# Attention with an MLP on one core: the turns of a step moved behind the second MLP unit of their gap, four idle matmuls removed

## The chip, the cores and the metric

One core of one Trainium2 chip. Times are device microseconds (us) of one execution, as the median of several. In a trace, PE is TensorE (PEld its weight loads), DVE is VectorE, ACT is ScalarE, POOL is GpSimd. Shorter is better; a difference under 2% counts as "same".

## The reference

Eight batches, twelve heads, 448 tokens, head size 64. Queries and keys are normalised, attention is taken, the heads are joined and go through an MLP.

```python
q_n, k_n = rmsnorm(q, g_q), rmsnorm(k, g_k)              # (8, 12, 448, 64)
attn = softmax(q_n @ k_n.T / 8)
x = (attn @ v).transpose(0, 2, 1, 3).reshape(3584, 768)
h = x @ w_in                                             # 768 -> 2048
g = max(h, 0) + alpha * min(h, 0)
out = g @ w_out                                          # 2048 -> 768, float32
```

## The kernel before

The heads of a batch are done in three steps of four heads, so there are 24 steps (y = 0 to 23). A step has seven score tiles. The program is a hand-made order of 66 bursts: each issues two or three score tiles with their exponentials, at times the denominators (`den`) or the outputs (`attv`) of an earlier step, and is followed by a gap that holds MLP units of an earlier batch: `up` (6 matmuls into one bank, then gT = max(h, alpha h) by ScalarE and VectorE) and `down` (16 matmuls). The order of the program is the order on each engine.

A *turn* makes a step's keys ready. Up to step 7, TensorE transposes q and k, and VectorE copies both out of PSUM, the memory that TensorE writes. From step 8 on DMAs have transposed them, and the turn is one VectorE instruction that scales kT in place:

```python
def turn(y):
    if y >= TD:                                   # TD = 8
        t = qkT[y, "k"].rearrange("p j g c -> p (j g c)")
        nc.vector.tensor_scalar(                  # 128x896 fp16, SBUF to SBUF (L179)
            out=t, in0=t, scalar1=gain[:, 0:1], scalar2=None, op0=ALU.mult
        )
        return
    ...                                           # 14 transposes (L193), then
    ...                                           # qT by a copy (L202), kT scaled by gain (L204)

def square(y, nm):                                # of a later step, by GpSimd
    ...
    nc.gpsimd.tensor_mul(out=sqf, in0=src, in1=src)                    # L135

def scale(y, nm):                                 # of a later step, mostly by GpSimd
    ...
    eng.tensor_mul(out=..., in0=nat[y, nm], in1=rr_t[y]...)            # qs, L158
```

The loop over bursts, as far as it matters (n is the burst; `turns[n]` is the step whose turn lies in its gap, mostly one burst before that step's first score):

```python
for n in range(NB):
    ...                                           # scores, exponentials, den / attv
    for k, (f, a) in enumerate(gaps[n]):
        spare = k == spare_at                     # this unit goes into the accumulator's banks
        if f is down:
            down(*a, jobs.pop(n, ()), spare)
        else:
            f(*a, spare)
            ...
        if k == 0 and n in turns:
            turn(turns[n])
    if not gaps[n] and n in turns:
        turn(turns[n])
    ...
    if n < first and plain and n not in turns:    # first = 12
        spin(4)                                   # four matmuls on zeros, to keep TensorE busy
    elif lead and n in dens:
        spin(8)
```

## Time and profile before

| | kernel before |
|---|---|
| time, median of 3 | 453.33 us (452.82 to 453.57) |
| PE busy in the profiled run | 426.9 of 451.6 us |
| ACT, DVE, POOL busy | 290.0, 207.8, 171.2 us |
| granted TensorE clock | 0.999 |

(The profiled run, 453.43 us, is a further one.)

TensorE is busy nearly all the time, so its waits are what to look for. The list of waits of the kernel before has these rows for the keys (columns: who waited, for whom; us in total, times, longest):

```profile
PEld L217 <- DVE kT L204: 4.0, 4, 1.3
PE sc L217 <- DVE kT L204: 3.2, 4, 1.0
PEld L217 <- DVE kT L179: 0.5, 1, 0.5
```

The first two are the opening's, where each step's keys are made just in time. Of the 16 turns that only scale kT (L179), one made a weight load wait, for half a microsecond.

### The profile page before, as it was taken

To read this page: it belongs to the slowest core of one execution; us is meant where nothing else is said; L and a number is where in the kernel's file an instruction comes from. 1 tells how busy PE (TensorE), PEld (TensorE's weight loads), DVE (VectorE), ACT (ScalarE), POOL (GpSimd) and SP (SyncE) were. 2 spreads that over 40 slices of the span, in tenths; PEclk is the share of its full clock that TensorE was granted. 3 is DMA by queue.
4 is the path that set the end of the run, shared out by engine and by line. 5 is a ranking of instruction groups with operands and counts; after the bars stand their busy time and mean duration, and the time that the engine had idled before them with its cause. 6 is when DMAs were issued, how large, how long until landed. Compare 5 with 4: busy or idle time off the path is not lost.

```text
span 451.6 us, 9099 instructions
## 1 busy us (share of the span) xinstructions
PE 426.9 (95%) x3848; PEld 230.0 (51%) x3848; DVE 207.8 (46%) x297; ACT 290.0 (64%) x401; POOL 171.2 (38%) x125
## 2 busy tenths in 40 slices
PE   8768989899999999999999999999999999999996
PEld 3334544555445545455545545455555555455563
DVE  3655553635463544444563544444563343343421
ACT  4998789557875848558785848558785846423300
POOL 5779952751472350750572350750542000000000
PEclk9999999999999999999999999999999999999999
DMA  8999995484655642764664642764361510111122
GB/s 191 233 247 241 232 240 117 60 168 110 158 94 127 159 105 53 140 156 118 157 109 111 158 107 53 139 157 118 77 100 38 77 37 1 37 35 36 35 71 70
DMA packets 60009, 52.77 MB, mean 117 GB/s; under 512 B 32688, under 2 KB 56512, under 8 KB 59968
## 3 DMA queue, kind: packets, MB, share of 16 engines
q1 hardware_dynamic: 47424, 39.27, 36.9%
q0 software_dynamic: 11808, 11.81, 16.7%
q10 hardware_dynamic: 736, 1.11, 1.0%
q8 instruction: 30, 0.49, 0.5%
q14 instruction: 11, 0.09, 0.1%
HBM read 45.62 MB, written 11.01 MB: 125 GB/s over the span
## 4 chain that ended last, share of the span: by engine, by line
PE 79%; ACT 14%; DVE 4%; DMA 1%; issue 1%; SPq 0%; ACTq 0%
PE op L301 31%; PE hT L284 18%; PE hTa L284 9%; ACT expT L229 8%; PE sc L217 7%; PE av L240 5%; PE dn L240 5%; ACT ah L292 2%; PE opa L301 2%; ACT rden L255 2%; DVE gT L293 2%; ACT rden L260 1%; DMA nat<-in_k_dram 1%; PE tps L193 1%; DVE ss L141 1%
## 5 line engine op out<-in xcount | busy, mean ns | idle before, releaser
L229 ACT ACTIVATE expT<-sc,expb 128x896 f16<-128x896 f32 x168 | 157.6, 1008 | 18.9 <-PE sc L217 18.7
L301 PE MATMUL op<-w_out_sb,gT 128*128 128x384 f16 x848 | 145.9, 326 | 2.1 <-DVE gT L293 2.0
L158 POOL TENSOR_TENSOR qs<-nat,rr 128x896 f16<-128x896 f32 x44 | 78.3, 1799 | 177.7 <-issue 159.0
L284 PE MATMUL hT<-xT,w_in_sb 128*128 128x448 f16 x558 | 117.1, 353 | 2.7 <-DVE gT L293 2.6
L301 PEld LDWEIGHTS <-gT 128*128 128x128 f16 x896 | 84.6, 98 | 65.5 <-issue 12.3
L284 PEld LDWEIGHTS <-w_in_sb 128*128 128x128 f16 x768 | 73.7, 98 | 72.8 <-issue 8.5
L292 ACT ACTIVATE ah<-hT,cols 128x448 f16<-128x448 f32 x93 | 59.1, 636 | 59.5 <-PE hT L284 59.4
L293 DVE TENSOR_TENSOR gT<-hT,ah 128x448 f16<-128x448 f32 x93 | 58.0, 624 | 76.5 <-ACT ah L292 76.5
L135 POOL TENSOR_TENSOR sq<-nat 128x896 f32<-128x896 f32 x44 | 73.0, 1681 | 1.4 <-DMA nat<-in_q_dram 1.3
L313 DVE COPY osb<-op 128x384 f32<-128x384 f32 x53 | 29.5, 557 | 89.4 <-PE op L301 89.4
L217 PE MATMUL sc<-qT,kT 64*64 64x448 f16 x672 | 53.2, 359 | 9.5 <-ACT expT L229 6.0
L292 ACT ACTIVATE ah<-hTa,cols 128x448 f16<-128x448 f32 x35 | 22.2, 633 | 49.5 <-PE hTa L284 49.5
L141 DVE TENSOR_REDUCE ss<-sq 128x14 f32<-128x896 f32 x48 | 49.8, 1076 | 6.5 <-ACT sq L133 6.1
L284 PE MATMUL hTa<-xT,w_in_sb 128*128 128x448 f16 x210 | 45.4, 352 | 0.0
L217 PEld LDWEIGHTS <-kT 64*64 64x64 f16 x672 | 19.2, 104 | 39.1 <-issue 29.0
L240 PE MATMUL av<-expT,vt 64*64 64x448 f16 x672 | 36.0, 350 | 2.2 <-ACT rden L255 2.2
L293 DVE TENSOR_TENSOR gT<-hTa,ah 128x448 f16<-128x448 f32 x35 | 21.8, 623 | 31.3 <-ACT ah L292 31.3
L240 PE MATMUL dn<-expT,ones 64*64 64x448 f16 x672 | 35.9, 349 | 0.2 <-DVE gT L293 0.2
L268 DVE TENSOR_TENSOR xT<-av,rden 128x896 f16<-128x896 f32 x24 | 26.2, 1090 | 20.7 <-PE av L240 20.7
L240 PEld LDWEIGHTS <-vt 64*64 64x64 f16 x672 | 20.3, 107 | 14.3 <-issue 3.7
L240 PEld LDWEIGHTS <-ones 64*64 64x64 f16 x672 | 20.5, 107 | 11.9 <-issue 1.0
L260 ACT ACTIVATE rden<-rden 128x896 f32<-128x896 f32 x24 | 23.0, 957 | 0.6
(37 smaller groups left out, 134.0 us busy)
## 6 DMA issues: line engine op xcount, KB each, us to landing
out_dram<-osb SPq DMA_DIRECT2D x54, 192.0 KB, 2.7
nat<-in_q_dram SPq DMA_DIRECT2D x46, 224.0 KB, 6.1
nat<-in_k_dram SPq DMA_DIRECT2D x46, 224.0 KB, 6.9
vt<-in_v_dram POOLq DMA_DIRECT2D x16, 336.0 KB, 7.6
w_in_sb<-in_moe_w_in_dram POOLq DMA_DIRECT2D x4, 768.0 KB, 13.2
w_out_sb<-in_moe_w_out_dram POOLq DMA_DIRECT2D x4, 768.0 KB, 16.6
nat<-in_q_dram ACTq DMA_DIRECT2D x2, 224.0 KB, 4.6
nat<-in_k_dram ACTq DMA_DIRECT2D x2, 224.0 KB, 6.1
```

What stands on the lines that cost most here:

```text
L135: nc.gpsimd.tensor_mul(out=sqf, in0=src, in1=src)
L141: nc.vector.tensor_reduce(out=ss_t[y][:, "qk".index(nm)].rearrange("p h j -> p (h j)").unsqueeze(2), in_=sqs[y, nm], axis=AXIS_X, op=ALU.add,)
L158: eng.tensor_mul(out=t.rearrange("p j h d -> p h j d"), in0=nat[y, nm], in1=rr_t[y][:, "qk".index(nm)].unsqueeze(3).broadcast_to((128, 2, ...
L217: nc.tensor.matmul(out=sc[ds(64 * g, 64), par, :S].rearrange("p (j c) -> p j c", j=J), lhsT=kT[ds(64 * par, 64), j, g, :], rhs=qT[ds(64 * ...
L229: nc.scalar.activation(out=expT[y][:, j], in_=scs[y, j][:, :, :S], func=AF.Exp, scale=QK_SCALE, bias=expb[:, 0:1],)
L240: nc.tensor.matmul(out=acc[ds(64 * par, 64), g, :S], lhsT=weights(g, par, j), rhs=e[ds(64 * g, 64), j, par, :], start=(j == 0), stop=(j == ...
L260: nc.scalar.activation(out=r, in_=r, func=AF.Exp, scale=-1.0)
L284: nc.tensor.matmul(out=hT[:, :S], lhsT=w_in_sb[:, c, ts(ft, 128)], rhs=x[:, c, :], start=(c == order[0]), stop=(c == order[-1]),)
L292: nc.scalar.activation(out=ah, in_=hT[:, :S], func=AF.Copy, scale=alpha_sb[:, ft : ft + 1])
L293: nc.vector.tensor_max(out=gT[:, ft, ds((b & 1) * S, S)], in0=hT[:, :S], in1=ah)
L301: nc.tensor.matmul(out=op[:, :OH], lhsT=gT[:, ft, ts(t, 128)], rhs=w_out_sb[:, ft, ds(oh * OH, OH)], start=(ft == 0), stop=(ft == NF - 1),)
L313: nc.vector.tensor_copy(out=o[:, ds(oh * OH, OH)], in_=op[:, :OH])
```

## The change

The intent, as the change states it: let the first units of a gap go ahead of the turn, and do away with idle matmuls where TensorE is about to do the third group's denominators.

```diff
-            if k == 0 and n in turns:
-                turn(turns[n])
+            if k == min(1, len(gaps[n]) - 2) or len(gaps[n]) == 1:
+                if n in turns:
+                    turn(turns[n])
         if not gaps[n] and n in turns:
             turn(turns[n])
         for _, g, c in late:
             g(*c)
-        if n < first and plain and n not in turns:
+        if n < den_at[G - 1] - 1 and plain and n not in turns:
             spin(4)
```

A gap of three or more units now has its turn behind the second; a gap of two keeps it behind the first. The second edit takes out one group of four idle matmuls, that of burst 10.

## The prediction

> **What bounds the kernel now.** The program runs in bursts of two or three score tiles, each followed by a gap that holds MLP units (up: 6 matmuls, down: 16) and at times the turn of a step, which readies its keys. I read the page's chain first, then TensorE's timeline, then VectorE's and GpSimd's beside it. The chain that ended last:
>
> ```profile
> PE 79%; ACT 14%; DVE 4%; DMA 1%; issue 1%; SPq 0%; ACTq 0%
> ```
>
> TensorE holds 79% of it, and PE is busy 426.9 of 451.6 us. In its timeline nearly all its pauses lie before 127 us (the opening and the first bursts with MLP work, where ScalarE's exponentials lead) or near 385. From 127 to 385 us it runs almost without a gap, so there anything that makes TensorE wait goes into the total. One of the change's 14 moved places, as the trace has it: step 10 of 24 (eight batches, three groups of heads each; TensorE, then VectorE, then GpSimd):
>
> ```profile
> 142.44 2.77 PE L301 MATMUL op<-w_out_sb,gT 128*128 128x384 f16 x16
> 145.05 1.30 PE L284 MATMUL hTa<-xT,w_in_sb 128*128 128x448 f16 x6
> 146.18 1.30 PE L284 MATMUL hT<-xT,w_in_sb 128*128 128x448 f16 x6
> 147.41 0.57 PE L217 MATMUL sc<-qT,kT 64*64 64x448 f16 x8
> ```
>
> ```profile
> 145.25 0.56 DVE L313 COPY osb<-op 128x384 f32<-128x384 f32 x1 [1.72 <-PE op L301]
> 145.73 0.47 DVE L179 TENSOR_SCALAR kT<-kT,gain 128x896 f16<-128x896 f16 x1
> 147.05 0.62 DVE L293 TENSOR_TENSOR gT<-hTa,ah 128x448 f16<-128x448 f32 x1 [0.86 <-ACT ah L292]
> 148.19 0.62 DVE L293 TENSOR_TENSOR gT<-hT,ah 128x448 f16<-128x448 f32 x1 [0.51 <-ACT ah L292]
> ```
>
> ```profile
> 144.25 3.48 POOL L158 TENSOR_TENSOR qs<-nat,rr 128x896 f16<-128x896 f32 x2 [10.52 <-issue]
> 147.70 3.31 POOL L135 TENSOR_TENSOR sq<-nat 128x896 f32<-128x896 f32 x2
> ```
>
> The gap is one down unit and two up units, then the scores at 147.41, which read this kT. The turn of a step from 8 on is only VectorE's scaling of kT. It stands behind the down unit, is done at 146.19, and the scores have 1.2 us to spare. It fills VectorE's idle time before gT, which waits for ScalarE either way.
>
> **What the Trainium skill says.** "SBUF — State Buffer", Who interferes with whom: VectorE's second port pair is GpSimd's, taken exclusively for a whole instruction; tensor_scalar in a two-port mode takes it, and the other "fully blocks". The trace agrees closely:
>
> ```profile
> L179 DVE TENSOR_SCALAR kT<-kT,gain x16: 445/658/975, 112.9 to 362.9; 128x896 f16<-128x896 f16 x16
> ```
>
> The 445 ns is the one where GpSimd is idle. The others (466, 658, 971) start at different points within the first qs, but all end 0.25 us after that qs ends (145.94 to 146.19; 127.31 to 127.56), and the second qs then takes 1837 instead of 1687 ns. "VectorE: DVE Perf Modes", Mode 4×_2P: four elements a cycle for this form; 896 / 4 / 0.96 GHz = 233 ns, the 0.25 us. "TensorE: Matmul & The Clock Gate", Part 3, The mechanism: matmuls start in strict program order, so a score that waits holds all behind it; TensorE's timeline shows no overtaking. The same page, Part 1: the clock falls after an idle window of about 3.4 us; granted clock here is 1.00 from 134 to 236 us, and no new wait that I expect reaches that.
>
> **The change part by part.** The order of VectorE's instructions confirms: of the gaps with three or more units, 14 hold a turn; 13 of them move one kT scaling behind one more gT, and step 4 moves 14 transposes and two copies. Gaps of two units or none are as before. All other engines keep their order, except the four idle matmuls taken out.
>
> *Idle matmuls (39 us).* They cost 0.86 us on the chain, but what follows does not only wait for them:
>
> ```profile
> 38.99 0.93 PE L328 MATMUL spin<-idle,ident 128*128 128x448 f16 x4
> 39.85 1.52 PE L240 MATMUL dn<-expT,ones 64*64 64x448 f16 x28
> 40.64 0.32 ACT L152 ACTIVATE rr<-ss,epsb 128x28 f32<-128x28 f32 x1 [0.52 <-DVE ss L141]
> 40.99 0.23 ACT L153 ACTIVATE rr<-rr 128x28 f32<-128x28 f32 x1
> 41.42 0.92 ACT L255 ACTIVATE rden<-dn 128x896 f32<-128x896 f32 x1 [0.20 <-PE dn L240]
> ```
>
> The logarithm of the denominators (41.42) stands behind the two root instructions, which wait for VectorE's sums and end at 41.22. It can move up 0.2 us at most: **-0.2 us**.
>
> *Step 4 (51 to 56 us).* Now: transposes 51.62, qT 53.03, kT 53.56, scores 54.77. After: the second unit takes the transposes' place; its gT comes at 53.92 (ah behind the exponential that ends 53.35), qT 0.54 later, kT 0.54 after that, done 55.67, scores 55.72: 0.95 late. The exponential behind them starts at 55.41 now (behind ah of the third unit) and would start 0.43 after the scores, 56.15. From here ScalarE's chain leads: **+0.7**.
>
> *Steps 10, 12, 14, 16, 18, 20, 22* (scores first in the next burst). kT follows gT by 0.54 us (126.05 to 126.59 at step 9) and takes 0.445 if free; TensorE resumes 0.045 later. Step 10: 147.05 + 0.54 + 0.445 + 0.045 = 148.08 against 147.41, +0.67. But GpSimd must be asked. qs starts at 144.25, its second ends 147.59 when nothing disturbs it, and the square starts 147.55; kT starts at 147.586. From the waits above I work out, as an estimate, that kT needs the ports some 0.2 us after its recorded start and a GpSimd instruction 0.14 us after its own. So the square has them 0.09 us earlier, and kT waits until it ends, 149.22, + 0.25: scores at 149.52, **+2.1**. Step 16 has the same distances (qs 245.84, gT 248.64): +2.1. At steps 12, 14, 18 and 20 gT comes 2.60 us after qs instead of 2.80, and kT asks just as the second qs ends: +0.67 each; for 12 and 18 the down unit of the next gap already waits 1.02 us for gT behind the exponentials, so only their delay, about 0.47, counts. Step 22 meets no later GpSimd work: +0.67. Sum 2×2.1 + 2×0.47 + 3×0.67 = **+7.1**.
>
> *Steps 11, 17, 23* (scores second in the burst, 0.2 us later). gT 161.04 gives kT done 162.02, scores 162.07 against 161.60: 3×0.46 = **+1.4**.
>
> *Steps 9, 15, 21* (gap of up units). One or two units still follow the turn, so alone it costs nothing. At 15 kT would start at 228.58, against 228.55 of the second qs: loses the ports by the same 0.08 us, ends 230.24 + 0.25, scores 230.54 against 229.74: +0.8; step 21 the same. Step 9 starts 0.07 ahead of the qs and wins by a hair: 0. **+1.6**.
>
> Sum: -0.2 + 0.7 + 7.1 + 1.4 + 1.6 = +10.6 us on 453.3: 463.9. The gT that come up to 0.7 us sooner gain nothing: where TensorE waits for gT (126.7, 189.0), it is one ahead of the turn or behind ScalarE.
>
> **The rivals.**
> (a) The same delays, but kT gets the ports at steps 10, 15, 16 and 21, my margin being 0.08 us from two recorded starts and an estimated offset. Then 2×0.67 in place of 2×2.1 and 0 for 1.6: +6.2, 459.5 us. For it: recorded starts of GpSimd are rough. Against it: distances that repeat to 10 ns at steps 10 and 16.
> (b) Step 9 loses the ports too: +1.1, 465.0.
> (c) It gains: the idle matmuls' 0.86 us is wholly given back and gT, sooner, frees the hT banks. For it: they are on the chain of waits. Against it: the roots end 0.2 us ahead of the logarithm, and bank waits of moved gaps are before the turn. It would make 452.5.
> (d) The delays are caught up later by slack. Against it: TensorE is gapless where they fall. With half absorbed: 458.5.
>
> **Range and chances.** 2% is 462.4 us. I give my base case with or without (b) some 0.63, (a) 0.3 with mixtures near the line, (c) 0.01. Predicted 463.6, pulled a little down by (a); range 459.0 to 465.4. Faster 0.01, same 0.37, slower 0.62.
>
> **What would show it.** Right: a new wait of the score's weight load for kT L179, about 12 times, 7 to 11 us in total; two of some 2.1 us, two of 0.8, the rest 0.45 to 0.67; kT scalings of about 1.9 us at steps 10, 15, 16 and 21; the logarithm no more than 0.2 us sooner; score waits for kT L204 grown by one near 55 us. Wrong in size: kT there at 0.45 us means (a). Wrong in mechanism: kT waits present but the span not longer by their sum means (d); no kT waits at all means that I misread which burst needs which kT. A granted clock below 1.00 would be something that I did not foresee.

## The result, and the profile after

| | before | changed |
|---|---|---|
| time, median of 4 | 453.25 us (452.82 to 453.57) | 466.13 us (464.12 to 466.94) |
| profiled span | 451.6 us | 465.1 us |
| granted clock | 0.999 (the profiled run) | 0.987 (profiled), 1.000, 0.991, 0.993 |

The ratio is 1.0278, 95% interval 1.0243 to 1.0313: slower. The direction and the mechanism were foreseen, but 466.13 lies above the stated range, which ended at 465.4. The run at full clock, 464.12 us, is where the prediction had put the kernel (463.9 before a small pull down).

The chain that ended last, and the rows of waits for kT, of the changed kernel:

```profile
PE 74%; ACT 14%; DVE 8%; issue 1%; DMA 1%; SPq 0%; ACTq 0%
```

```profile
PEld L217 <- DVE kT L179: 14.2, 13, 2.5
PE sc L217 <- DVE kT L179: 9.3, 12, 2.0
PEld L217 <- DVE kT L204: 5.5, 5, 1.3
PE sc L217 <- DVE kT L204: 4.2, 5, 1.0
```

TensorE lost five points of the chain and VectorE gained four. The scores waited 12 times for L179, 9.3 us in all, where before no matmul did, and a fifth time for L204 (step 4). The rows of step 10, in the order of those in the prediction (TensorE, VectorE, GpSimd):

```profile
146.58 1.30 PE L284 MATMUL hTa<-xT,w_in_sb 128*128 128x448 f16 x6
147.71 1.30 PE L284 MATMUL hT<-xT,w_in_sb 128*128 128x448 f16 x6
151.06 0.57 PE L217 MATMUL sc<-qT,kT 64*64 64x448 f16 x8 [2.04 <-DVE kT L179]
```

```profile
148.58 0.62 DVE L293 TENSOR_TENSOR gT<-hTa,ah 128x448 f16<-128x448 f32 x1 [1.25 <-ACT ah L292]
149.12 1.88 DVE L179 TENSOR_SCALAR kT<-kT,gain 128x896 f16<-128x896 f16 x1
150.92 0.61 DVE L293 TENSOR_TENSOR gT<-hT,ah 128x448 f16<-128x448 f32 x1
```

```profile
145.78 3.33 POOL L158 TENSOR_TENSOR qs<-nat,rr 128x896 f16<-128x896 f32 x2 [10.44 <-issue]
149.07 3.46 POOL L135 TENSOR_TENSOR sq<-nat 128x896 f32<-128x896 f32 x2
```

kT starts at 149.12, 0.05 us after GpSimd's first square, and takes 1.88 us instead of 0.47. The pair of squares takes 3.46 us instead of 3.31, and the two qs 3.33 instead of 3.48: the 0.15 us that kT costs GpSimd has moved from one pair to the other. TensorE stands still for 2.04 us.

To compare places, I took the start of every score tile's first matmul in both traces and the places where the difference of the two jumps. Beside the prediction's terms:

| place | predicted | measured in the changed kernel's trace |
|---|---|---|
| step 4 | scores 0.95 late, +0.7 net | +0.95, then -0.19: +0.76 |
| steps 10, 16 | +2.1 each | +2.12, +2.12 |
| steps 12, 18 | +0.47 each | +0.68, then -0.19: +0.49 each |
| steps 14, 20, 22 | +0.67 each | +0.68 each |
| steps 11, 17, 23 | +0.46 each | +0.47 each |
| steps 15, 21 | +0.8 each | +0.80, +0.79 |
| step 9 | 0 | 0 (kT 442 ns) |
| four idle matmuls gone | -0.2 | -0.99, +0.29, +0.38: -0.32 |
| sum of these | +10.6 | +10.7 |
| right behind step 16's wait | nothing | +1.63 more |

The last row is what the prediction had not: after step 16's scores the tiles fall behind by another 0.44 and 1.19 us although nothing waits. The busy times of two stretches of 3.4 us (columns: busy us and count of PE, PEld, DVE, ACT, POOL; then the granted clock, DMA share, GB/s) and two from the opening tell why:

```profile
26.40:29.80 3.40, 1.66 (x22) 1.01 (x21) 2.34 (x4) 2.98 (x4) 3.40 (x3) 1.00 1.21 244
29.80:33.20 3.40, 3.37 (x40) 1.65 (x43) 2.29 (x3) 2.34 (x4) 2.04 (x4) 0.50 1.15 254
255.10:258.50 3.40, 1.35 (x29) 0.82 (x32) 3.40 (x4) 1.46 (x2) 3.40 (x3) 1.00 0.77 144
258.50:261.90 3.40, 3.40 (x27) 1.34 (x20) 1.21 (x2) 2.90 (x5) 0.23 (x1) 0.50 1.00 248
```

In the stretch with the wait TensorE is busy for 1.35 of 3.40 us, and in the next one it runs at half its clock. The clock record of this run has three such stretches before the end, from 12.75, 29.81 and 258.51 us, each of 3.413 us and at whole multiples of 3.413 from each other. Step 16's wait, from 255.2 to 257.24 us, lies wholly within the stretch before the last of them; step 10's began 0.26 us before such a stretch did (149.28 us), so that TensorE was busy for 1.63 us of it, and the next one kept its clock. The page shows them as digits below 9 in its clock row:

```profile
PEclk9889999999999999999999899999999999999999
```

### The profile page after: what moved, and what is told of

Its sections match the earlier page's. It is cut to its first block, busy times and chain, and to the rows that moved or that the text cites. A ratio compares the mean times of both kernels' runs of the same rounds, so it can differ in the third digit from the quotient of the medians.

```text
span 465.1 us, 9091 instructions
## 1 busy us (share of the span) xinstructions
PE 431.1 (93%) x3844; PEld 229.7 (49%) x3844; DVE 210.4 (45%) x297; ACT 291.1 (63%) x401; POOL 170.5 (37%) x125
## 4 chain that ended last, share of the span: by engine, by line
PE 74%; ACT 14%; DVE 8%; issue 1%; DMA 1%; SPq 0%; ACTq 0%
PE op L301 31%; PE hT L284 15%; PE hTa L284 8%; PE sc L217 7%; ACT expT L229 7%; PE dn L240 5%; PE av L240 5%; ACT ah L292 4%; DVE gT L293 3%; DVE kT L179 2%; PE opa L301 2%; ACT rden L255 2%; ACT rden L260 1%; DMA nat<-in_k_dram 1%; DVE ss L141 1%
## 5 line engine op out<-in xcount | busy, mean ns | idle before, releaser
L158 POOL TENSOR_TENSOR qs<-nat,rr 128x896 f16<-128x896 f32 x44 | 76.8, 1765 | 190.9 <-issue 176.6
L135 POOL TENSOR_TENSOR sq<-nat 128x896 f32<-128x896 f32 x44 | 74.0, 1703 | 1.1 <-DVE kT L204 1.0
L217 PE MATMUL sc<-qT,kT 64*64 64x448 f16 x672 | 55.2, 369 | 19.1 <-DVE kT L179 9.3
L240 PE MATMUL dn<-expT,ones 64*64 64x448 f16 x672 | 37.7, 362 | 0.2 <-DVE gT L293 0.2
L255 ACT ACTIVATE rden<-dn 128x896 f32<-128x896 f32 x24 | 22.2, 926 | 1.7 <-PE dn L240 1.7
```

The costliest lines, as they stand in the source:

```text
L158: eng.tensor_mul(out=t.rearrange("p j h d -> p h j d"), in0=nat[y, nm], in1=rr_t[y][:, "qk".index(nm)].unsqueeze(3).broadcast_to((128, 2, ...
L217: nc.tensor.matmul(out=sc[ds(64 * g, 64), par, :S].rearrange("p (j c) -> p j c", j=J), lhsT=kT[ds(64 * par, 64), j, g, :], rhs=qT[ds(64 * ...
L240: nc.tensor.matmul(out=acc[ds(64 * par, 64), g, :S], lhsT=weights(g, par, j), rhs=e[ds(64 * g, 64), j, par, :], start=(j == 0), stop=(j == ...
L255: nc.scalar.activation(out=r, in_=rden[y][:, :, :S], func=AF.Ln)
```

## The experiments

Each was run in five rounds against the kernel before. Kernels are compared only within the same rounds. All gave correct results. By the 2% rule moved_only, fill_pauses, both_fill and squares_wait are slower, all others "same". The kernel before took 453.74 us (453.10 to 454.81, 11 runs) in the first call with four kernels, 453.48 (453.15 to 454.22, 11 runs) in the second, 453.71 (the first call's runs and one more) and 453.50 in the last two. Its runs have granted clocks from 0.991 to 1.000, so it too has half-clock stretches at times: of the runs in the first two calls, those at 0.998 or more took 453.10 to 453.72, the others 453.18 to 454.81.

### moved_only: the turns moved, the idle matmuls kept

```diff
-        if n < den_at[G - 1] - 1 and plain and n not in turns:
+        if n < first and plain and n not in turns:
             spin(4)
```
(against the changed kernel)

> The turns moved, the four idle matmuls kept: only the second part of the change is undone. My theory: the kT waits are the whole loss and the idle matmuls are worth 0.2 us, so runs at a granted clock of 1.00 take 464.1 to 464.5 us (changed kernel's clean run 464.12), with kT at 1.88 us for steps 10 and 16 and 1.90 us for 15 and 21; half-clock windows after the pause of step 10 or 16 stay possible and make some runs 465.5 to 467. Rival: the missing idle matmuls cause the lower clock and what the prediction fell short by; then every run is at 1.00 and near 463.9.

Measured: 464.56 us (463.98 to 465.97), ratio 1.0239 (1.0218 to 1.0260). The jumps of all steps are those of the table within 0.02 us. The run at clock 1.000 took 463.98, the three at 0.994 took 464.42, 464.69 and 465.97. The turns are the loss, and half-clock stretches occur with the idle matmuls in place: the rival, that taking them out caused the lower clock, falls.

### spins_only: the idle matmuls removed, the turns where they were

```diff
-        if n < first and plain and n not in turns:
+        if n < den_at[G - 1] - 1 and plain and n not in turns:
             spin(4)
```
(against the kernel before)

> The four idle matmuls removed, the turns left behind the first unit. My theory: the logarithm of the denominators moves up 0.2 us and no more, 453.1 us against 453.25, same within noise, and granted clock as in the kernel before. Rival: TensorE idle at 40 us lets its clock fall to one half for a window, and the kernel loses 0.5 to 1.5 us, 454 to 455, in some runs with a half-clock window between 38 and 48 us.

Measured: 453.25 us (452.73 to 454.21), ratio 0.9987 (0.9972 to 1.0002): same. In the profiled run no half-clock stretch lies between 38 and 48 us; it had one from 29.8 us, which is ahead of where the removed matmuls stood, so their absence can't be its cause.

### four_back: the turns of steps 10, 15, 16 and 21 put back

```diff
-            if k == min(1, len(gaps[n]) - 2) or len(gaps[n]) == 1:
+            own = 0 if turns.get(n) in (10, 15, 16, 21) else min(1, len(gaps[n]) - 2)
+            if k == own or len(gaps[n]) == 1:
```

> The changed kernel with the turn of steps 10, 15, 16 and 21 put back behind the first unit. My theory: these four hold the ports conflicts, worth 2 x 2.12 + 2 x 0.80 = 5.84 us in the changed kernel's trace, and the only pauses above 1 us, so 458.3 us in all runs, no kT scaling above 1.0 us, and no half-clock window after 100 us. Rival: the delay is spread evenly over the 14 places, then 4 of 14 put back give 3.1 us, 461.0; or half-clock windows come from something else and still appear near 150 or 258 us.

Measured: 459.51 us (458.82 to 459.87), ratio 1.0120 (1.0099 to 1.0141). The run with the highest clock, 0.999, took 458.82; the others, at 0.991 to 0.995, 459.43 to 459.87. In its profile no kT scaling is longer than 0.98 us, no half-clock stretch starts between 34 us and the end of the matmuls, and these four jumps are gone while the others stay at their sizes. Against the changed kernel's 464.12 at full clock that is 5.3 us less (5.84 expected, which is also what the four jumps sum to), and far from the 3.1 of an even spread. That all runs would be at 458.3 did not come true: the profiled run had a half-clock stretch at 30.0 us, behind which its score tiles stayed 0.9 us late.

### fill_pauses: idle matmuls in the two long waits

```diff
         sc = pss.tile([128, 2, 512], FP32, name="sc", tag="sc")
+        if (y, j) in ((10, 0), (16, 0)):
+            for _ in range(10):
+                nc.tensor.matmul(
+                    out=sc[:, 0, :S], lhsT=ident, rhs=idle, start=True, stop=True
+                )
```
(against the changed kernel)

> The changed kernel with ten idle matmuls (about 1.9 us) in front of the first scores of steps 10 and 16, in the score tile itself, where TensorE would wait for kT. My theory: the time not explained by waits comes from half-clock windows that follow a 3.4 us window in which TensorE is busy for less than about half; filled pauses take these away, so all runs are at 464.0 to 464.5 but for half-clock windows before 40 us, and none shows one after 100 us. Rival: the pauses have nothing to do with the clock: the spread 464.1 to 466.9 stays, with windows near 150 or 258 us; or idle matmuls delay the scores and the time rises.

Measured: 464.23 us (463.71 to 464.48), ratio 1.0226 (1.0208 to 1.0243). Its profile has no half-clock stretch before the end, and kT of steps 10 and 16 still takes 1.88 us. The stretch with step 16's wait and the one behind it (columns as above):

```profile
253.28:256.69 3.41, 3.26 (x30) 1.57 (x31) 3.22 (x4) 1.10 (x3) 3.41 (x3) 1.00 0.71 135
256.69:260.10 3.41, 3.41 (x46) 1.88 (x35) 1.72 (x2) 3.38 (x5) 0.74 (x1) 1.00 0.93 239
```

No run reaches 465, so the fill costs little or nothing. By itself this profile proves little, since those of moved_only and squares_wait have no half clock behind the two waits either; the run times of this test and the next are what tells. A low clock alone isn't a loss: the fastest run here had 0.994.

### both_fill: the opening filled too

```diff
+    def fill(count):                     # matmuls on zeros, into the accumulator's banks
+        ...
+    fill(3)
     turn(0)
+    fill(4)
...
+        if n in turns and turns[n] < G:  # steps 1 and 2
+            fill(2 * turns[n])
```
(with fill_pauses' edit)

> The changed kernel with both sets of idle matmuls: the opening's, and ten ahead of the first scores of steps 10 and 16. My theory: what the prediction fell short by (2.2 us) is half-clock windows alone, so all runs lie at 463.7 to 464.3, granted clock 1.00 but for the last microseconds. Rival: some runs still reach 466, then waits that the profiled run does not show are the cause.

Measured: 464.36 us (464.17 to 464.59), granted clocks 0.998 to 1.000, ratio 1.0238 (1.0224 to 1.0251). Two of the four runs, 464.44 and 464.59, lie a little above the range expected. So with TensorE kept busy the changed kernel takes 463.71 to 464.59 us in all eight runs of these two kernels. Without, the twelve runs of the changed kernel, moved_only and squares_wait (below) go from 463.98 to 466.94, median 465.5.

### open_fill: the opening's fill in the kernel before

The same four fills, without anything else.

> The kernel before with idle matmuls (3, 4, 2 and 4) where TensorE waits for the first three steps' keys, into the free accumulator. My theory: the spread of the kernel before (452.8 to 454.8) comes from half-clock windows in the first 35 us, which follow a window with TensorE busy for less than about half; with the pauses filled all runs lie within 452.6 to 453.6 and no half-clock window shows before 400 us. Rival: the spread has another source (DMA arrival at the start) and stays, or the idle matmuls delay the first scores, 453.5 to 454.5.

Measured: 453.63 us (453.20 to 453.97), ratio 1.0000 (0.9988 to 1.0012). Its clocks are 0.997 to 1.000, where the kernel before had 0.991 to 1.000, so the low clocks are gone; but its five runs lie no lower than those of the kernel before at full clock (453.10 to 453.72), and three of them (453.63, 453.64, 453.97) lie above what was expected. For the time it is inconclusive.

### squares_wait: a test that tested nothing

```diff
+            if turns.get(n - 2) in (10, 16):      # wrong bursts: no square is held
+                held.setdefault(turns[n - 2], []).append((y, nm))
```

> The changed kernel, but GpSimd's two squares of the bursts where step 10 and step 16 turn wait (through a one-element VectorE write to their tile) until kT is scaled. My theory, ports taken whole: kT of steps 10 and 16 takes 0.45 instead of 1.88 us, the scores wait 0.67 instead of 2.12, so 2.9 us less than the changed kernel: 461.2 us at full clock, no half-clock window after 100 us; steps 15 and 21 keep 1.90 us. Rival: kT is slow there for another reason (a late DMA of kT, a busy VectorE), then it stays at 1.9 us and the time at 464.1 or more.

Measured: 465.49 us (464.43 to 466.00), ratio 1.0259 (1.0246 to 1.0272), kT of step 10 still 1.88 us. I had held the squares written in those bursts; the ones that run there are written two bursts later and start as soon as GpSimd is free. None matched, and the instructions of every engine are those of the changed kernel, in the same order. So it says nothing of the theory, and stands here as a second sample of the changed kernel: 465.49 after 466.13.

### squares_wait2: GpSimd's squares held until kT is scaled

```diff
         sq = ld.tile([128, 2 * J, D], FP32, name="sq", tag="sq", bufs=4)
         sqf = sq.rearrange("p n d -> p (n d)")
+        if hold:
+            nc.vector.memset(sqf[:, 0:1], 0.0)    # VectorE, behind the kT scaling
...
+            for a in held.pop(y, ()):             # in turn(), y = 10 and 16
+                square(*a, hold=True)
```
(against the changed kernel; now the right squares)

> As squares_wait was meant: there the hold caught no square (the squares that run in those bursts are written two bursts later in the program), so it ran as the changed kernel. Now GpSimd's two squares behind qs of the bursts where steps 10 and 16 turn wait, through a one-element VectorE write to their tile, until kT is scaled. My theory, ports taken whole by whoever asks first: kT of steps 10 and 16 takes 0.45 instead of 1.88 us, the scores wait about 0.67 instead of 2.12, so 2.9 us less than the changed kernel's clean 464.1 to 464.4: 461.2 to 461.6 us, and no half-clock window after 100 us; steps 15 and 21 keep 1.90 us. Rival: kT is slow there for another reason (its DMA, a busy VectorE), then it stays at 1.9 us and the time at 464.1 or more.

Measured: 461.40 us (461.02 to 462.19), ratio 1.0168 (1.0152 to 1.0184). VectorE and GpSimd at step 10 (in this kernel L181 is the kT scaling and L137 the squares):

```profile
147.20 0.62 DVE L297 TENSOR_TENSOR gT<-hTa,ah 128x448 f16<-128x448 f32 x1 [1.24 <-ACT ah L296]
147.75 0.44 DVE L181 TENSOR_SCALAR kT<-kT,gain 128x896 f16<-128x896 f16 x1
148.14 0.07 DVE L133 MEMSET sq<- 128x1 f32 x2
```

```profile
144.40 3.33 POOL L160 TENSOR_TENSOR qs<-nat,rr 128x896 f16<-128x896 f32 x2 [10.43 <-issue]
148.35 3.31 POOL L137 TENSOR_TENSOR sq<-nat 128x896 f32<-128x896 f32 x2 [0.61 <-POOL qs L160]
```

Only the squares' start has moved, by 0.6 us, and kT takes 0.44 instead of 1.88. The jumps of steps 10 and 16 are 0.68 each, as at the steps without a conflict; steps 15 and 21, where nothing was held, keep a kT of 1.90 us. So what made kT slow there is GpSimd's instruction beside it.

### only_step4: only that turn moved

```diff
-            if k == 0 and n in turns:
+            if k == (1 if turns.get(n) == 4 else 0) and n in turns:
                 turn(turns[n])
```
(against the kernel before)

> The kernel before with only step 4's turn (transposes and two copies) moved behind the second unit. My theory: the scores of step 4 come 0.95 later, 0.2 of it hides behind the exponentials, so +0.75 us: 454.0 against 453.25, or 454.5 against 453.75 where half-clock windows fall in the opening of both. Rival: the opening is led by ScalarE and absorbs it: +0.0 to +0.2.

Measured: 454.21 us (453.91 to 456.61), ratio 1.0023 (1.0005 to 1.0041), against 453.48: +0.73 by the medians. The opening does not absorb it. One run of six took 456.61, at a clock of 0.990.

### more_banks: a try at beating both

```diff
+        allup = n in avs and all(f is up for f, _ in gaps[n])
-        for k, (f, a) in enumerate(gaps[n][:-1]):
-            free = 2.3 if n in dens else 1.2 if n in avs else 0.1
+        for k, (f, a) in enumerate(gaps[n] if allup else gaps[n][:-1]):
+            free = 2.2 if n in dens else 1.2 if n in avs else 0.1
```
(against spins_only; it moves four up units into the accumulator's banks)

> A try at beating both kernels: the turns where the kernel before has them, the four idle matmuls gone, and four up units (the third of bursts 12, 24, 25 and 64) in the free accumulator instead of a bank of the MLP pair that TensorE waits for (0.25, 0.85 and 0.77 us in the trace of the kernel before, and one near 386 us). My theory: the waits at 118.9 and 126.7 us go, as TensorE leads there, the one at 48.7 is ScalarE's and stays: 1.6 us less from those, 0.2 from the idle matmuls: 451.5 to 452.0 us against 453.3 to 453.7, same by 2%. Rival: the next user of the accumulator (the following denominators or outputs) then waits for the unit's gT in turn, and nothing or half of it is left: 452.5 to 453.5.

Measured: 450.51 us (450.25 to 451.90), ratio 0.9935 (0.9921 to 0.9948). By the 2% rule that is "same", but the interval is clear of 1: it is the fastest kernel here, 3 us below the kernel before and some 14 below the changed one at full clock. TensorE about burst 24, before:

```profile
115.61 2.44 PE L284 MATMUL hT<-xT,w_in_sb 128*128 128x448 f16 x12
118.91 2.66 PE L284 MATMUL hT<-xT,w_in_sb 128*128 128x448 f16 x12 [0.85 <-DVE gT L293]
```

and in more_banks:

```profile
116.50 2.44 PE L284 MATMUL hT<-xT,w_in_sb 128*128 128x448 f16 x12
118.78 1.30 PE L284 MATMUL hTa<-xT,w_in_sb 128*128 128x448 f16 x6
119.91 1.30 PE L284 MATMUL hT<-xT,w_in_sb 128*128 128x448 f16 x6
```

The third unit goes into the accumulator (hTa) and follows without a wait. It gained more than the expected 1.8 us. By the jumps of the score tiles, the four units gave 0.41 (burst 12, where I had expected nothing), 1.10, 0.70 and, by what the spans differ after the last score, 0.60 us, 2.8 in all; the rest is about what the idle matmuls were worth.

## Why the prediction was wrong

It fell outside its range by 0.7 us at the median. Step by step:

- **What bounds the kernel** held: from 127 to 385 us each new wait of TensorE went into the total, but for the 0.19 us that steps 12 and 18 each gave back, as foreseen. Rival (d), slack that catches up the delays, falls.
- **The places and sizes of the waits** held, nearly to the hundredth, in the table above. moved_only and four_back show the same jumps when parts are undone.
- **The ports** held: the four predicted losses of the race at steps 10, 15, 16 and 21 occurred, step 9 won, and holding the squares (squares_wait2) took the extra 1.4 us off steps 10 and 16. Rivals (a) and (b) fall. At step 9 that was partly luck: by the prediction's own estimate (VectorE needs the ports 0.2 us after its recorded start, GpSimd 0.14) a lead of 0.07 us left 0.01 to spare. Its 233 ns for the ports' share of the kT scaling is an estimate, from figures of the Trainium skill's "VectorE: DVE Perf Modes", Mode 4×_2P and the clock on that page; in the traces kT ends 0.25 us behind GpSimd's instruction each time that it had to wait.
- **The idle matmuls** held: "It can move up 0.2 us at most", and in squares_wait2, whose opening had full clock, the logarithm follows the end of step 3's kT by 0.31 us less than before (40.84 - 38.35 = 2.49, against 41.42 - 38.62 = 2.80). A little more than 0.2, since the logarithm's record begins 0.1 us before that of the root instruction in front of it ends:

```profile
40.71 0.23 ACT L155 ACTIVATE rr<-rr 128x28 f32<-128x28 f32 x1
40.84 0.90 ACT L259 ACTIVATE rden<-dn 128x896 f32<-128x896 f32 x1
```

Rival (c) falls, since the kernel did not gain. Whether the idle matmuls were worth 0.2 or 0.86 us the times can't tell (spins_only's 0.13% is 0.6 us, its interval -0.1 to 1.3); the score tiles do, which in spins_only too come 0.32 us sooner once they are gone.

- **The step that failed** is the one on the clock: "the clock falls after an idle window of about 3.4 us; granted clock here is 1.00 from 134 to 236 us, and no new wait that I expect reaches that." I took idle to mean wholly idle, and noted only that a clock below 1.00 would be unforeseen. The runs show that a stretch in which TensorE was busy for 1.35 of 3.4 us, with a wait of 2.05, was followed by one at half clock, and this cost 1.63 us (0.44 + 1.19) in the profiled run. The stretches lie on a fixed grid of 3.413 us that is not tied to the program, so the same wait falls within one stretch in one run and over two in the next. In the profiled run step 16 was hit and step 10 was not; in those of moved_only and squares_wait neither was.
- **A second part of the shortfall is not the change's.** In the profiled run two more half-clock stretches, at 12.7 and 29.8 us, lie before any instruction that differs, and six of the other eleven profiled kernels had one or both. Compared with squares_wait2, which had none and started alike (0.25 and 0.28 us earlier than before), the changed kernel is 1.37 us later at burst 12. What such a stretch costs depends on its place: alone at 13.4 us nothing (moved_only, only_step4), alone at 29.8 us 0.9 us (spins_only). The kernel before has low clocks in some runs too. Low clocks were not bad luck in the first four runs: ten of the twelve runs of the changed kernel, moved_only and squares_wait have 0.987 to 0.996. Where on the grid a run falls is luck, and with it the median; the second sample of the changed kernel had 465.49.

The check of the cause is the pair of filled kernels: with matmuls on zeros in the pauses all eight runs lie at 463.71 to 464.59, from 0.2 below to 0.7 us above the predicted sum of 463.9. That the stretch at step 16 cost 1.63 us is read from the trace; that the pauses bring such stretches rests on filling them: none of the eight filled runs is over 464.6, seven of the twelve others are over 465. How the shortfall of the unfilled runs splits between the two long waits and the opening is shown for the profiled run alone. fill_pauses fills only the two waits, and its runs were as low; with four runs I can't say how much of that was the grid.

In short: the sum was right for full clock, and the range left out a mode that a wait of two microseconds can set off.

## What to carry to other kernels

An instruction moved later on an engine with slack is free only up to its reader: find the reader's place, and count what now stands between. Here the move spent 1.2 us of slack for nothing, since the gT that came sooner were not what TensorE waited for. For a VectorE instruction that takes the ports it shares with GpSimd, as kT's scaling does, look at what GpSimd does at that moment: kT won when its record began 0.065 us ahead and lost when it began 0.03 us behind, so less than 0.1 us decided over 1.4 us. And where TensorE stands still for most of a 3.4 us stretch, allow for half clock in the next, or fill the pause with matmuls that nothing reads.

## What the Trainium skill lacked or had wrong

- "TensorE: Matmul & The Clock Gate", Part 1 and the section "Why this matters for your kernels", ties the half clock to an idle window and to idle gaps above some 3 us. Here a gap of 2.05 us was enough (busy 1.35 of 3.4 us, next stretch at 0.50), and so were two opening stretches of the changed kernel with no gap above 0.92 us (busy 1.66 and 1.70 of 3.4); a passage of Part 1 on a second failure mode allows for frequent short idles, but gives no figure. I lack one too, but the twelve traces narrow it down. Laid on the grid of each one's clock record, from 7 to 440 us, 14 stretches had TensorE busy for 1.74 us or less; ten of them (1.37 to 1.74) were followed by one at half clock. Of the 1506 stretches busy for 1.86 us or more none was. The four exceptions had 1.58 to 1.73, so the busy time that a trace shows, whose matmul ends are modelled, is no exact threshold. The page's window of 3413 ns, free-running, agrees with the clock records.
- "SBUF — State Buffer", Who interferes with whom, was right on all that was tested: exclusive, for the whole instruction, decided by who asks first (kT 0.44 or 1.88 us by the squares' start alone). It does not say how asking relates to the recorded start: kT lost when its record began 0.03 to 0.05 us after that of GpSimd's instruction, and at step 9 won with its record 0.065 us ahead.
- No page that I read says what a GpSimd instruction pays when VectorE goes between two of its own: 0.15 us here (1687 to 1837 ns).
